# A transformer block on one core: where the first projections get their normalized rows, and when

## The chip, the cores and the metric

The kernel runs on one core of one Trainium2 chip. Its engines are TensorE (PE, matmuls; PEld is its weight load), VectorE (DVE), ScalarE (ACT), GpSimd (POOL) and SyncE (SP, which here only issues DMAs). The metric is device time in microseconds (us), the median of several executions; lower is better.

## What is computed

A layer norm of x (2048 rows of 448) feeds two branches whose sums are added to x: attention with 16 heads of 28 columns that share one k and one v, and an MLP with a hidden width of 1792.

```python
xn = _layernorm(x, axis=-1)                     # (x - mean) / sqrt(var + 1e-5)
q = (xn @ wq).reshape(B, S, 16, 28).transpose(0, 2, 1, 3)
k, v = xn @ wk, xn @ wv                         # one head for all
p = softmax(einsum("bhqd,bkd->bhqk", q, k) * 28 ** -0.5)
o = einsum("bhqk,bkd->bhqd", p, v).transpose(0, 2, 1, 3).reshape(B, S, 448)
return x + o @ wo + relu(xn @ w1) @ w2
```

## The kernel before

All arithmetic is in 32 bits. Most matmul operands are split into a high and a low part of TensorE's rounded 32-bit format (names that end in H and L, or hi and lo), and a product is the sum of three of the four partial products.

The 2048 rows are taken as four blocks of 512 (NQB = 4), each of four tiles of 128 rows (TPB). The kernel runs in three stages, one after the other: first layer norm and the q, k and v projections of the four blocks, then the MLP (from L436 on), then attention (from L593 on). The change lies in the first stage, L76 to L320. For a block b that stage does this:

- moments(b) (L196): DVE takes mean and variance of the four x tiles in acc, by four pairs of instructions (L200, L201).
- rstd(b) (L204): ACT takes a square root (L208), and DVE makes 1/sqrt(variance) from it in six small instructions (L209 to L214); nb, the last one, is what ACT's normalization adds.
- normalized_x(b) (L217): the four tiles are normalized, tiles 0 and 2 on DVE (L229), tiles 1 and 3 on ACT (L227). POOL copies the last 64 columns of each a second time (L232), which only the last chunk's transposes need.
- transposed(b) (L236): PE transposes the block, chunk by chunk (DC = 3 chunks of 128 columns and the doubled rest of 64; four transposes for a chunk, L241), into PSUM tiles named d, of which there are three, and o for the rest. ACT copies each chunk out as its high part xH (L243), DVE subtracts to get the low part xL (L244); the rest goes to xR by two copies on ACT and a subtraction on DVE (L247 to L249).
- qkv_proj(b, g) for four groups of heads g (L258): eleven matmuls of 512 columns (L187, L192) into a PSUM tile named a, of which there are four; then qkv_out (L251): ACT copies the result (L254), DVE subtracts (L255), and SP writes it to a scratch tensor in HBM (L256).

Block 0 is treated on its own: qkv_first (L263) does its four groups side by side in 44 matmuls, pass by pass through the chunks (L271), the passes with low weights last, and only then the four qkv_out. Its weights come from HBM as they are (wq by L116 to L120, wk and wv by L118 to L120, all issued by SP) and are split on the chip: high parts on ACT (split_hi, L146), low parts on POOL for chunks 0 and 2 and on DVE for chunks 1 and 3 (split_lo, L151).

While PE has no data, 28 warm-up matmuls of an identity run on it (L97; each stands as two instructions in the trace).

The order in which the functions are called in L278 to L319 is written out by hand, and it sets the order of the instructions of every engine. Before the change, block 1's moments, rstd and normalized_x are called ahead of qkv_first, and transposed(1) behind it. In the loop over b, moments(b + 1) stands ahead of the block's first projection, rstd(b + 1) behind it, normalized_x(b + 1) behind the second, transposed(b + 1) behind the third. SP issues the four tiles of block 0, then wq, wk, wv, then the twelve remaining x tiles (L137), and later the first MLP weights (load_part, L155), which POOL splits (split_part, L165) during block 2.

Of the kernel before, what the change touches and what calls it, by code (L numbers as in the profile page):

```python
# [8 lines left out]
F32 = mybir.dt.float32  # L9
F32R = mybir.dt.float32r  # L10
I32 = mybir.dt.int32
AF = mybir.ActivationFunctionType
ALU = mybir.AluOpType
# [25 lines left out]
def program(ctx: ExitStack, tc: tile.TileContext, HM, fine, x, wq, wk, wv, wo, w1, w2, out):  # L39
    nc = tc.nc  # L40
    P = 128
    S, D = x.shape
# [19 lines left out]
    WARM = 28  # L62
# [32 lines left out]
    pw = psD.tile([P, QB], F32, name="d")  # L95
# [16 lines left out]
    def chunks_in(dst, src, each=False):  # L112

        if each:
            for c in range(DC):
                nc.sync.dma_start(dst[:, c], src[c * P : (c + 1) * P])  # L116
        else:
            nc.sync.dma_start(dst[:, 0:DC], src[0 : DC * P].rearrange("(c p) n -> p c n", p=P))  # L118
        nc.sync.dma_start(dst[0:DR, DC], src[DC * P : D])
        nc.sync.dma_start(dst[DR:P, DC], src[DC * P : D])  # L120
# [9 lines left out]
    with nc.allow_non_contiguous_dma(reason="narrow k and v projections"):  # L130
        chunks_in(kvs[:, :, 0:DH], wk)
        chunks_in(kvs[:, :, DH : 2 * DH], wv)
# [11 lines left out]
    def split_hi(c, kv):  # L144
        src, hi, lo = wqkv_parts(c, kv)
        nc.scalar.activation(hi, src, AF.Copy)  # L146

    def split_lo(c, kv):
        src, hi, lo = wqkv_parts(c, kv)
        eng = nc.vector if c % 2 else nc.gpsimd  # L150
        eng.tensor_tensor(lo, src, hi.bitcast(F32), op=ALU.subtract)  # L151
# [42 lines left out]
    stat = {}  # L194

    def moments(b):  # L196
        mv = small.tile([P, TPB, 2], F32, name="mv")
        for i in range(TPB):
            st = small.tile([P, 6], F32, name="st")
            nc.vector.bn_stats(st, acc[:, b * TPB + i, :])  # L200
            nc.vector.bn_aggr(mv[:, i, :], st)  # L201
        stat[b] = mv

    def rstd(b):  # L204

        mv = stat[b]
        ve, sd, r0, t0, rs, nb = (small.tile([P, TPB], F32, name=k) for k in ("ve", "sd", "r0", "t0", "rs", "nb"))
# [7 lines left out]
        stat[b] = mv, rs, nb  # L215

    def normalized_x(b):  # L217

        mv, rs, nb = stat.pop(b)
        xn = []  # L220
        for i in range(TPB):
            if i % 2 == 0:
                pair = hpool.tile([P, FC, QB], F32, name="hL" if i else "hH")
            n = pair[:, i % 2]
            a = acc[:, b * TPB + i, :]
            if i % 2:
                nc.scalar.activation(n[:, 0:D], a, AF.Identity, bias=nb[:, i : i + 1], scale=rs[:, i : i + 1])  # L227
            else:
                nc.vector.tensor_scalar(  # L229
                    n[:, 0:D], a, mv[:, i, 0:1], rs[:, i : i + 1], op0=ALU.subtract, op1=ALU.mult  # L230
                )
            nc.gpsimd.tensor_scalar(n[:, D : D + DR], n[:, DC * P : D], 1.0, 0.0, op0=ALU.mult, op1=ALU.add)  # L232
            xn.append(n)
        return xn

    def transposed(b, xn, chunks=range(DC + 1)):  # L236
        xs = slice(b * QB, (b + 1) * QB)
        for c in chunks:
            pt = psD.tile([P, QB], F32, name="d") if c < DC else psO.tile([P, QB], F32, name="o")
            for i in range(TPB):  # L240
                nc.tensor.transpose(pt[:, i * P : (i + 1) * P], xn[i][:, c * P : (c + 1) * P], ident)  # L241
            if c < DC:
                nc.scalar.activation(xH[:, c, xs], pt, AF.Copy)  # L243
                nc.vector.tensor_tensor(xL[:, c, xs], pt, xH[:, c, xs].bitcast(F32), op=ALU.subtract)  # L244
            else:
                tmp = small.tile([P, QB], F32R, name="tmp")
                nc.scalar.activation(xR[0:DR, xs], pt[0:DR], AF.Copy)  # L247
                nc.scalar.activation(tmp[DR:P], pt[DR:P], AF.Copy)
                nc.vector.tensor_tensor(xR[DR:P, xs], pt[DR:P], tmp[DR:P].bitcast(F32), op=ALU.subtract)  # L249
# [31 lines left out]
    split_hi(1, False)  # L281
    xn = normalized_x(0)
    split_hi(0, True)
    split_hi(1, True)
    split_lo(1, False)
    split_lo(1, True)
    transposed(0, xn, (0, 1))
    split_hi(2, False)
    split_hi(2, True)
    transposed(0, xn, (2, 3))  # L290
    split_hi(3, False)
    split_hi(3, True)
    for c in (0, 2, 3):
        split_lo(c, False)
        split_lo(c, True)
    moments(1)
    rstd(1)
    xn = normalized_x(1)
    qkv_first(range(NHG))
    g0 = load_part(0)  # L300
    g1 = load_part(1)
    transposed(1, xn)
    for b in range(1, NQB):
        if b + 1 < NQB:
            moments(b + 1)
        qkv_proj(b, 0)
        if b + 1 < NQB:
            rstd(b + 1)
        qkv_proj(b, 1)
        if b + 1 < NQB:  # L310
            xn = normalized_x(b + 1)
        else:
            nc.scalar.activation(warm, eps_t, AF.Exp)
        qkv_proj(b, 2)
        if b + 1 < NQB:
            transposed(b + 1, xn)
        if b == 2:
            split_part(0, g0)
        qkv_proj(b, 3)  # L319
# [340 lines left out]
```

## Time and profile before

| | us |
|---|---|
| median of 3 runs | 883.08 (882.75 to 883.5) |
| the profiled execution, its own time | 882.62 |
| its span, first to last instruction | 880.8 |
| first stage, to the first MLP matmul | 58.83 |

The profile is of one execution. In its timeline a row is: start in us, busy time in us, engine, line, operation, output <- input, shapes, count, and in brackets the idle time of that engine just before and what ended it. SPq is SP's queue of DMA issues. In the table of windows a row is: the window, its length, then for each engine busy us and the number of instructions, then the granted clock of TensorE, the busy share of the DMA engines and GB/s. In a row of groups the figures behind the bar are busy us in total and mean ns of one. Matmuls are pipelined; where the text follows PE closely it goes by the starts of its weight loads (PEld).

### The profile page before, as it was taken

To read this page: it belongs to the slowest core of one execution; us is meant where nothing else is said; L and a number is where in the kernel's file an instruction comes from. 1 tells how busy PE (TensorE), PEld (TensorE's weight loads), DVE (VectorE), ACT (ScalarE), POOL (GpSimd) and SP (SyncE) were. 2 spreads that over 40 slices of the span, in tenths; PEclk is the share of its full clock that TensorE was granted. 3 is DMA by queue.
4 is the path that set the end of the run, shared out by engine and by line. 5 is a ranking of instruction groups with operands and counts; after the bars stand their busy time and mean duration, and the time that the engine had idled before them with its cause. 6 is when DMAs were issued, how large, how long until landed. Compare 5 with 4: busy or idle time off the path is not lost.

```text
span 880.8 us, 12946 instructions
## 1 busy us (share of the span) xinstructions
PE 871.0 (99%) x4998; PEld 573.0 (65%) x4998; DVE 471.0 (53%) x848; ACT 562.2 (64%) x871; POOL 113.3 (13%) x96
## 2 busy tenths in 40 slices
PE   9999999999999999999999999999999999999996
PEld 8788888888888886454554554554554554554562
DVE  6833344333333346474574574574574574574563
ACT  4541111111111116999999999999999999999993
POOL 3034202020202003010110110110110110110110
PEclk9999999999999999999999999999999999999998
DMA  6868050010000001020120230120230120230001
GB/s 214 293 200 167 4 132 23 23 45 1 1 1 1 0 2 38 2 56 25 33 56 21 57 77 21 36 56 20 58 77 15 42 56 17 62 77 14 2 13 46
DMA packets 37502, 45.89 MB, mean 52 GB/s; under 512 B 13640, under 2 KB 24072, under 8 KB 37264
## 3 DMA queue, kind: packets, MB, share of 16 engines
q1 hardware_dynamic: 37432, 44.98, 19.7%
q8 instruction: 41, 0.67, 0.3%
q14 instruction: 29, 0.24, 0.1%
HBM read 32.37 MB, written 12.18 MB: 51 GB/s over the span
## 4 chain that ended last, share of the span: by engine, by line
PE 98%; DVE 1%; ACT 1%; issue 0%; POOL 0%; POOLq 0%
PE o L477 25%; PE a L588 19%; PE a L187 16%; PE a L423 12%; PE d L588 10%; PE d L522 4%; PE o L423 4%; PE a L192 4%; PE d L370 2%; PE a L271 1%; PE d L97 1%; PE d L241 1%; ACT p L623 0%; PE a L565 0%; DVE qs L255 0%
## 5 line engine op out<-in xcount | busy, mean ns | idle before, releaser
L610 DVE COPY p<-d 128x512 f32<-128x512 f32 x384 | 246.1, 686 | 161.7 <-PE d L588 142.1
L605 ACT ACTIVATE p<-a 128x512 f32<-128x512 f32 x640 | 317.1, 708 | 21.7 <-PE a L588 21.7
L477 PE MATMUL o<-p,vtile 128*32 128x512 f32 x2048 | 229.5, 594 | 0.0
L588 PE MATMUL a<-qst,kst 114*128 114x512 f32 x640 | 225.4, 407 | 0.0
L410 ACT ACTIVATE hH<-a 128x512 fp32r<-128x512 f32 x56 | 33.5, 598 | 235.9 <-PE a L192 235.9
L623 ACT ACTIVATE p<-p 128x2048 f32<-128x2048 f32 x96 | 183.1, 2131 | 0.0
L588 PEld LDWEIGHTS a<-qst,kst 114*128 114x128 f32 x640 | 120.0, 187 | 77.2 <-ACT p L605 28.1
L477 PEld LDWEIGHTS o<-p,vtile 128*32 128x32 f32 x2048 | 61.6, 109 | 144.1 <-issue 128.3
L588 PE MATMUL d<-qst,kst 114*128 114x512 f32 x384 | 145.8, 400 | 0.0
L187 PE MATMUL a<-xH,w 128*128 128x512 f32 x408 | 104.8, 392 | 0.2 <-ACT xH L243 0.2
L411 DVE SCALAR_TENSOR_TENSOR hL<-a,hH 128x512 fp32r<-128x512 f32 x56 | 38.7, 692 | 118.4 <-ACT hH L410 118.4
L423 PE MATMUL a<-w,hH 128*128 128x448 f32 x336 | 95.6, 366 | 0.0
L187 PEld LDWEIGHTS a<-xH,w 128*128 128x128 f32 x408 | 76.1, 188 | 16.5 <-ACT xH L243 0.8
L588 PEld LDWEIGHTS d<-qst,kst 114*128 114x128 f32 x384 | 72.4, 188 | 12.9 <-DVE p L610 4.5
L508 POOL TENSOR_TENSOR on<-rb,oS 128x512 f32<-128x512 f32 x15 | 19.4, 1290 | 448.4 <-DMA rb<-rscr 418.0
L430 DVE TENSOR_TENSOR acc<-a,acc 128x448 f32<-128x448 f32 x84 | 52.2, 622 | 33.7 <-PE a L423 33.7
L423 PEld LDWEIGHTS a<-w,hH 128*128 128x128 f32 x336 | 63.0, 188 | 6.3
L423 PE MATMUL a<-w,hL 128*128 128x448 f32 x168 | 61.2, 364 | 0.0
L187 PE MATMUL a<-xL,w 128*128 128x512 f32 x204 | 57.7, 390 | 0.1
L187 PEld LDWEIGHTS a<-xL,w 128*128 128x128 f32 x204 | 38.3, 188 | 8.8 <-DVE xL L244 0.7
L192 PE MATMUL a<-xR,w 128*128 128x512 f32 x136 | 42.0, 390 | 0.2 <-DVE xR L249 0.2
L524 DVE TENSOR_TENSOR acc<-d,acc 128x448 f32<-128x448 f32 x60 | 37.3, 622 | 5.3 <-PE d L522 5.3
(111 smaller groups left out, 577.4 us busy)
## 6 DMA issues: line engine op xcount, KB each, us to landing
qst<-qscr SPq DMA_DIRECT2D x64, 224.0 KB
qscr<-qs SPq DMA_DIRECT2D x16, 512.0 KB
rb<-rscr SPq DMA_DIRECT2D x60, 64.0 KB
acc<-in_A_x SPq DMA_DIRECT2D x16, 224.0 KB
out<-acc SPq DMA_DIRECT2D x16, 224.0 KB
stg<-in_B_w SPq DMA_DIRECT2D x7, 448.0 KB
stg<-in_B_w SPq DMA_DIRECT2D x7, 384.0 KB
qst<-rows SPq DMA_DIRECT2D x128, 2.0 KB
```

The costliest lines, as they stand in the source:

```text
L187: nc.tensor.matmul(ps, lhs[:, wi, c, cols], xm[:, c, xs], start=n == 0, stop=False)
L192: nc.tensor.matmul(ps, lhs[:, wi, DC, cols], xR[:, xs], start=False, stop=wi == 1)
L411: nc.vector.scalar_tensor_tensor(hL[:, f], ph, 0.0, hH[:, f].bitcast(F32), op0=ALU.max, op1=ALU.subtract)
L423: nc.tensor.matmul(py[:, 0:D], hm[:, f, i * P : (i + 1) * P], wd[:, wi, f, :], start=n == 0, stop=n == 3 * FC - 1)
L430: nc.vector.tensor_tensor(acc[:, t, :], py[:, 0:D], acc[:, t, :], op=ALU.add)
L477: nc.tensor.matmul(o_acc[u][32 * j : 32 * j + 32], vtile[:, kb, :], p[:, j], start=start, stop=stop)
L522: nc.tensor.matmul(py, om[:, c], wm[:, g, :], start=n == 0, stop=n == 2)
L524: nc.vector.tensor_tensor(acc[:, t, :], py, acc[:, t, :], op=ALU.add)
L588: nc.tensor.matmul(pt, kst[0 : KQ + 2, kb * P : (kb + 1) * P], qst[u][0 : KQ + 2, j, :], start=True, stop=True)
L605: nc.scalar.activation(p, pt, AF.Exp, scale=SCALE)
L610: nc.vector.tensor_copy(p, pt)
L623: nc.scalar.activation(ps[kb], ps[kb], AF.Exp, scale=SCALE)
```

## The change

- wk and wv are loaded by issues on ACT's queue, behind ACT's first instruction; wq stays on SP.
- 24 warm-up matmuls instead of 28, and they write to a PSUM tile named a instead of d.
- Block 0's tiles are normalized by DVE, ACT, DVE and POOL; the second copies of the 64 last columns come behind all four. The high part of wq's chunk 1 is made on DVE instead of ACT, and all low parts on POOL, behind block 0's transposes in the code. The high parts of chunks 2 and 3 are made between the chunks of block 0's transposes.
- Block 1's moments, rstd and normalized_x are called behind qkv_first instead of ahead of it, right before its transposed(1). Then come the loads of the first MLP weights and moments(2), rstd(2).
- In the loop, normalized_x(b + 1) stands ahead of the block's first projection, transposed(b + 1) behind the second, and behind that moments(b + 2) and rstd(b + 2).

transposed is cut into x_bank, turn and split_x, with the same instructions; the small tiles of the statistics are allocated in moments.

```diff
--- before.py
+++ after.py
@@ -59,7 +59,7 @@
     W2C = FC * D
     SCALE = float(DH) ** -0.5
     EPS = 1e-5
-    WARM = 28
+    WARM = 24
     KQ = 4 * DH
     NU = NQB * NHG
     NA, ND, NST = 4, 3, 3
@@ -92,7 +92,7 @@
     gone = cst.tile([P, TPB + 3], F32, name="gone")
     nc.vector.memset(gone, 1.0)
 
-    pw = psD.tile([P, QB], F32, name="d")
+    pw = psA.tile([P, QB], F32, name="a")
     for _ in range(WARM):
         nc.tensor.matmul(pw[:, 0:P], ident, ident, start=True, stop=True)
     kst = cst.tile([P, S], F32R, name="kst")
@@ -109,15 +109,15 @@
     proj_scope = ExitStack()
     npool = proj_scope.enter_context(tc.tile_pool(name="npool", bufs=1, side="right"))
 
-    def chunks_in(dst, src, each=False):
+    def chunks_in(dst, src, each=False, eng=nc.sync):
 
         if each:
             for c in range(DC):
-                nc.sync.dma_start(dst[:, c], src[c * P : (c + 1) * P])
+                eng.dma_start(dst[:, c], src[c * P : (c + 1) * P])
         else:
-            nc.sync.dma_start(dst[:, 0:DC], src[0 : DC * P].rearrange("(c p) n -> p c n", p=P))
-        nc.sync.dma_start(dst[0:DR, DC], src[DC * P : D])
-        nc.sync.dma_start(dst[DR:P, DC], src[DC * P : D])
+            eng.dma_start(dst[:, 0:DC], src[0 : DC * P].rearrange("(c p) n -> p c n", p=P))
+        eng.dma_start(dst[0:DR, DC], src[DC * P : D])
+        eng.dma_start(dst[DR:P, DC], src[DC * P : D])
 
 
     nc.scalar.activation(warm, eps_t, AF.Sqrt)
@@ -128,8 +128,8 @@
     kvs = stg[:, (DC + 1) * D : (DC + 1) * (D + 2 * DH)].rearrange("p (c n) -> p c n", c=DC + 1)
     chunks_in(s3, wq, each=True)
     with nc.allow_non_contiguous_dma(reason="narrow k and v projections"):
-        chunks_in(kvs[:, :, 0:DH], wk)
-        chunks_in(kvs[:, :, DH : 2 * DH], wv)
+        chunks_in(kvs[:, :, 0:DH], wk, eng=nc.scalar)
+        chunks_in(kvs[:, :, DH : 2 * DH], wv, eng=nc.scalar)
     wqkv = wpool.tile([P, 2, 4, 512], F32R, name="w")
     w4 = wqkv.rearrange("p s c (g n) -> p s c g n", g=NHG)
     nc.gpsimd.memset(w4[:, :, :, :, MQ + DHH : P].bitcast(F32), 0.0)
@@ -141,14 +141,16 @@
         cols = slice(MQ, MQ + DHH) if kv else slice(0, MQ)
         return src, w4[:, 0, c, :, cols], w4[:, 1, c, :, cols]
 
-    def split_hi(c, kv):
+    def split_hi(c, kv, eng=None):
         src, hi, lo = wqkv_parts(c, kv)
-        nc.scalar.activation(hi, src, AF.Copy)
+        if eng is None:
+            nc.scalar.activation(hi, src, AF.Copy)
+        else:
+            eng.tensor_copy(hi, src)
 
     def split_lo(c, kv):
         src, hi, lo = wqkv_parts(c, kv)
-        eng = nc.vector if c % 2 else nc.gpsimd
-        eng.tensor_tensor(lo, src, hi.bitcast(F32), op=ALU.subtract)
+        nc.gpsimd.tensor_tensor(lo, src, hi.bitcast(F32), op=ALU.subtract)
 
     parts = {}
 
@@ -191,20 +193,22 @@
         for wi in range(2):
             nc.tensor.matmul(ps, lhs[:, wi, DC, cols], xR[:, xs], start=False, stop=wi == 1)
 
-    stat = {}
+    stat, xns = {}, {}
 
     def moments(b):
-        mv = small.tile([P, TPB, 2], F32, name="mv")
+
+        stat[b] = tuple(
+            small.tile([P, TPB, 2] if k == "mv" else [P, TPB], F32, name=k)
+            for k in ("mv", "ve", "sd", "r0", "t0", "rs", "nb")
+        )
         for i in range(TPB):
             st = small.tile([P, 6], F32, name="st")
             nc.vector.bn_stats(st, acc[:, b * TPB + i, :])
-            nc.vector.bn_aggr(mv[:, i, :], st)
-        stat[b] = mv
+            nc.vector.bn_aggr(stat[b][0][:, i, :], st)
 
     def rstd(b):
 
-        mv = stat[b]
-        ve, sd, r0, t0, rs, nb = (small.tile([P, TPB], F32, name=k) for k in ("ve", "sd", "r0", "t0", "rs", "nb"))
+        mv, ve, sd, r0, t0, rs, nb = stat[b]
         nc.scalar.activation(sd, mv[:, :, 1], AF.Sqrt, bias=eps_t)
         nc.vector.tensor_scalar(ve, mv[:, :, 1], EPS, None, op0=ALU.add)
         nc.vector.reciprocal(r0, sd)
@@ -212,41 +216,50 @@
         nc.vector.tensor_tensor(t0, t0, ve, op=ALU.mult)
         nc.vector.scalar_tensor_tensor(rs, t0, 1.5, r0, op0=ALU.add, op1=ALU.mult)
         nc.vector.scalar_tensor_tensor(nb, mv[:, :, 0], -1.0, rs, op0=ALU.mult, op1=ALU.mult)
-        stat[b] = mv, rs, nb
-
-    def normalized_x(b):
-
-        mv, rs, nb = stat.pop(b)
-        xn = []
-        for i in range(TPB):
-            if i % 2 == 0:
-                pair = hpool.tile([P, FC, QB], F32, name="hL" if i else "hH")
-            n = pair[:, i % 2]
+
+    def normalized_x(b, by=(nc.vector, nc.scalar) * 2):
+
+        mv, rs, nb = stat[b][0], stat[b][5], stat[b][6]
+        xns[b] = [hpool.tile([P, FC, QB], F32, name=k) for k in ("hH", "hL")]
+        for i, eng in enumerate(by):
+            n = xns[b][i // 2][:, i % 2]
             a = acc[:, b * TPB + i, :]
-            if i % 2:
-                nc.scalar.activation(n[:, 0:D], a, AF.Identity, bias=nb[:, i : i + 1], scale=rs[:, i : i + 1])
+            if eng is nc.scalar:
+                eng.activation(n[:, 0:D], a, AF.Identity, bias=nb[:, i : i + 1], scale=rs[:, i : i + 1])
             else:
-                nc.vector.tensor_scalar(
+                eng.tensor_scalar(
                     n[:, 0:D], a, mv[:, i, 0:1], rs[:, i : i + 1], op0=ALU.subtract, op1=ALU.mult
                 )
+        for i in range(TPB):
+            n = xns[b][i // 2][:, i % 2]
             nc.gpsimd.tensor_scalar(n[:, D : D + DR], n[:, DC * P : D], 1.0, 0.0, op0=ALU.mult, op1=ALU.add)
-            xn.append(n)
-        return xn
-
-    def transposed(b, xn, chunks=range(DC + 1)):
+
+    def x_bank(c):
+        return psD.tile([P, QB], F32, name="d") if c < DC else psO.tile([P, QB], F32, name="o")
+
+    def turn(b, c, pt):
+
+        for i in range(TPB):
+            n = xns[b][i // 2][:, i % 2]
+            nc.tensor.transpose(pt[:, i * P : (i + 1) * P], n[:, c * P : (c + 1) * P], ident)
+
+    def split_x(b, c, pt):
+
         xs = slice(b * QB, (b + 1) * QB)
-        for c in chunks:
-            pt = psD.tile([P, QB], F32, name="d") if c < DC else psO.tile([P, QB], F32, name="o")
-            for i in range(TPB):
-                nc.tensor.transpose(pt[:, i * P : (i + 1) * P], xn[i][:, c * P : (c + 1) * P], ident)
-            if c < DC:
-                nc.scalar.activation(xH[:, c, xs], pt, AF.Copy)
-                nc.vector.tensor_tensor(xL[:, c, xs], pt, xH[:, c, xs].bitcast(F32), op=ALU.subtract)
-            else:
-                tmp = small.tile([P, QB], F32R, name="tmp")
-                nc.scalar.activation(xR[0:DR, xs], pt[0:DR], AF.Copy)
-                nc.scalar.activation(tmp[DR:P], pt[DR:P], AF.Copy)
-                nc.vector.tensor_tensor(xR[DR:P, xs], pt[DR:P], tmp[DR:P].bitcast(F32), op=ALU.subtract)
+        if c < DC:
+            nc.scalar.activation(xH[:, c, xs], pt, AF.Copy)
+            nc.vector.tensor_tensor(xL[:, c, xs], pt, xH[:, c, xs].bitcast(F32), op=ALU.subtract)
+        else:
+            tmp = small.tile([P, QB], F32R, name="tmp")
+            nc.scalar.activation(xR[0:DR, xs], pt[0:DR], AF.Copy)
+            nc.scalar.activation(tmp[DR:P], pt[DR:P], AF.Copy)
+            nc.vector.tensor_tensor(xR[DR:P, xs], pt[DR:P], tmp[DR:P].bitcast(F32), op=ALU.subtract)
+
+    def transposed(b):
+        for c in range(DC + 1):
+            pt = x_bank(c)
+            turn(b, c, pt)
+            split_x(b, c, pt)
 
     def qkv_out(b, g, pq):
         xs = slice(b * QB, (b + 1) * QB)
@@ -278,44 +291,45 @@
     moments(0)
     rstd(0)
     split_hi(0, False)
-    split_hi(1, False)
-    xn = normalized_x(0)
+    normalized_x(0, (nc.vector, nc.scalar, nc.vector, nc.gpsimd))
     split_hi(0, True)
     split_hi(1, True)
-    split_lo(1, False)
-    split_lo(1, True)
-    transposed(0, xn, (0, 1))
-    split_hi(2, False)
-    split_hi(2, True)
-    transposed(0, xn, (2, 3))
-    split_hi(3, False)
-    split_hi(3, True)
-    for c in (0, 2, 3):
+    split_hi(1, False, nc.vector)
+    for c in range(DC + 1):
+        pt = x_bank(c)
+        turn(0, c, pt)
+        split_x(0, c, pt)
+        if c in (0, 1):
+            split_hi(c + 2, False)
+            split_hi(c + 2, True)
+    for c in range(DC + 1):
         split_lo(c, False)
         split_lo(c, True)
-    moments(1)
-    rstd(1)
-    xn = normalized_x(1)
     qkv_first(range(NHG))
-    g0 = load_part(0)
-    g1 = load_part(1)
-    transposed(1, xn)
     for b in range(1, NQB):
+        if b == 1:
+            moments(1)
+            rstd(1)
+            normalized_x(1)
+            transposed(1)
+            g0 = load_part(0)
+            g1 = load_part(1)
+            moments(2)
+            rstd(2)
         if b + 1 < NQB:
-            moments(b + 1)
+            normalized_x(b + 1)
+        else:
+            nc.scalar.activation(warm, eps_t, AF.Exp)
         qkv_proj(b, 0)
-        if b + 1 < NQB:
-            rstd(b + 1)
         qkv_proj(b, 1)
         if b + 1 < NQB:
-            xn = normalized_x(b + 1)
-        else:
-            nc.scalar.activation(warm, eps_t, AF.Exp)
-        qkv_proj(b, 2)
-        if b + 1 < NQB:
-            transposed(b + 1, xn)
+            transposed(b + 1)
+        if b + 2 < NQB:
+            moments(b + 2)
+            rstd(b + 2)
         if b == 2:
             split_part(0, g0)
+        qkv_proj(b, 2)
         qkv_proj(b, 3)
     proj_scope.close()
 
```

## The prediction

> **What bounds the kernel now.** I read the page first: the engine totals, then the chain that ended last.
>
> ```profile
> PE 871.0 (99%) x4998; PEld 573.0 (65%) x4998; DVE 471.0 (53%) x848; ACT 562.2 (64%) x871; POOL 113.3 (13%) x96
> ...
> PE 98%; DVE 1%; ACT 1%; issue 0%; POOL 0%; POOLq 0%
> ```
>
> TensorE (PE) holds 98% of the chain. Whatever makes PE wait is paid in full; whatever another engine does in PE's shadow is free. The diff touches only the time before the MLP, so next I cut the span at the places where PE goes from one kind of work to the next, in the table of windows.
>
> ```profile
> 11.74:21.55 9.81, 9.81 (x46) 8.15 (x44) 8.03 (x23) 4.95 (x12) 2.68 (x7) 1.00 0.76 258
> 21.55:58.83 37.28, 36.63 (x182) 29.58 (x181) 26.28 (x59) 20.88 (x38) 8.13 (x11) 1.00 0.72 251
> ```
>
> The first row is qkv_first (44 matmuls), the second is blocks 1 to 3 (twelve projections, three sets of sixteen transposes) up to the first MLP matmul at 58.83. How little of the second row is waiting shows from the undisturbed pieces in the timeline:
>
> ```profile
> 44.59 0.37 PEld L241 LDWEIGHTS d<-ident,hH 128*128 128x128 f32 x2
> ...
> 46.45 1.23 PEld L187 LDWEIGHTS a<-xH,w 128*128 128x128 f32 x6
> ...
> 53.84 1.32 PEld L187 LDWEIGHTS a<-xH,w 128*128 128x128 f32 x6
> ...
> 58.83 1.32 PEld L187 LDWEIGHTS a<-xH,w 128*128 128x128 f32 x6
> ```
>
> A set of transposes is 46.45 - 44.59 = 1.86 us; 53.84 to 58.83 holds two projections, so 2.495 each. 12 x 2.495 + 3 x 1.86 = 35.5 of 37.28: blocks 1 to 3 contain 1.8 us of waits. That is the most this part of the change could win.
>
> **In what order the engines work.** Everything below rests on one question: does an engine take instructions in the order of the code? VectorE (DVE) answers it in block 1 to 2:
>
> ```profile
> 38.21 0.69 DVE L255 TENSOR_TENSOR qs<-a,qs 128x512 fp32r<-128x512 f32 x1 [1.16 <-ACT qs L254]
> ...
> 38.82 0.62 DVE L200 BATCH_NORM_STATS2 st<-acc 128x6 f32<-128x448 f32 x1
> ```
>
> DVE idled 1.16 us for a projection's output (L255), although the next block's statistics (L200) needed only x, which had long been in SBUF. They stand after that L255 in the code, and they ran after it. So order in the code is order on the engine.
>
> **The moved statistics of block 1: the main term.** Before, moments(1), rstd(1) and normalized_x(1) stand ahead of qkv_first. After, they stand behind it, and so behind its four qkv_out, whose copies and subtractions wait for qkv_first's last matmuls.
>
> ```profile
> 18.32 0.18 DVE L201 BATCH_NORM_AGGREGATE mv<-st 128x2 f32<-128x6 f32 x1
> ...
> 20.53 0.75 ACT L227 ACTIVATE hL<-acc,nb,rs 128x448 f32<-128x448 f32 x1
> 20.68 0.87 PEld L271 LDWEIGHTS a<-xR,w 128*128 128x128 f32 x4
> ...
> 21.33 2.06 ACT L254 ACTIVATE qs<-a 128x512 fp32r<-128x512 f32 x4
> ...
> 21.59 0.37 PEld L241 LDWEIGHTS d<-ident,hH 128*128 128x128 f32 x2
> ...
> 21.96 2.48 DVE L255 TENSOR_TENSOR qs<-a,qs 128x512 fp32r<-128x512 f32 x4 [1.28 <-ACT qs L254]
> ...
> 27.00 0.63 DVE L200 BATCH_NORM_STATS2 st<-acc 128x6 f32<-128x448 f32 x1
> ...
> 29.84 0.18 DVE L201 BATCH_NORM_AGGREGATE mv<-st 128x2 f32<-128x6 f32 x1
> ```
>
> Now: block 1 is normalized at 21.28 (20.53 + 0.75), under the matmuls, and PE passes from qkv_first (20.68 + 0.87 = 21.55) straight to the transposes at 21.59. I call 21.33, where ScalarE (ACT) takes the first finished projection, E. After the change the links from E run in series:
>
> - DVE's four subtractions end at 21.96 + 2.48 = 24.44, E + 3.11.
> - moments(1) (eight instructions, 27.00 to 30.02 in the next block): 3.02, so E + 6.13.
> - rstd(1) and the four normalizations, from the last aggregate's end (18.50) to ACT's last tile (21.28): 2.78, so E + 8.91.
>
> PE stands still from E + 0.22 to about E + 8, against nothing now.
>
> **Block 2, which now comes behind two projections instead of three.** More rows, from block 0's transposes and block 2's splits:
>
> ```profile
> 9.54 0.75 ACT L227 ACTIVATE hL<-acc,nb,rs 128x448 f32<-128x448 f32 x1
> ...
> 10.34 0.14 PEld L241 LDWEIGHTS d<-ident,hL 128*128 128x128 f32 x1 [0.18 <-ACT hL L227]
> ...
> 10.82 1.06 ACT L243 ACTIVATE xH<-d 128x512 fp32r<-128x512 f32 x2
> ...
> 11.71 2.59 PEld L271 LDWEIGHTS a<-xH,w 128*128 128x128 f32 x12
> ```
>
> ```profile
> 33.68 1.58 ACT L243 ACTIVATE xH<-d 128x512 fp32r<-128x512 f32 x3
> ...
> 36.35 0.69 DVE L249 TENSOR_TENSOR xR<-o,tmp 64x512 fp32r<-64x512 f32 x1
> ```
>
> From the last normalized tile (10.29) to the first copy out of the transposes (10.82) is at most 0.53; I take 0.48: E + 9.39. From there to the end of the last split, 33.68 to 37.04, is 3.36: E + 12.75. DVE then does moments(2), 3.02, and rstd(2) with normalized_x(2), 2.78: E + 18.55. PE meanwhile ends its transposes at 8.91 + 0.05 + 1.37 (10.34 to 11.71) = E + 10.33, and two projections, with about 0.35 of waiting for the last split, at E + 15.7. It waits some 2.9 us for block 2's tiles: the third projection that covered this now comes behind. The transposes end at 18.55 + 0.05 + 1.37 = E + 19.97. What PE still has is ten projections and block 3's transposes, 24.95 + 1.86: E + 46.78.
>
> Is block 3 late too? PE reaches it at E + 19.97 + 9.98 = E + 29.95. After block 2's tiles ACT must first do the two queued copies (L254, 2.06 / 4 = 0.5 each), so the splits start at E + 19.6 and end at 22.9, moments(3) at 26.0, and rstd, two held L255 of 0.69 and the normalizations end near E + 29.8 to 30.1. It just fits; 0 to 0.4 us, taken as 0. POOL's weight split for the MLP (L168) follows block 3's tiles at about 51 us and has until 67 us.
>
> **The start.**
>
> ```profile
> 1.36 8.71 PE L97 MATMUL d<-ident 128*128 128x128 f32 x56 [1.36 <-POOL ident masks.py:199]
> ...
> 2.03 0.20 ACT L123 ACTIVATE warm<-eps_t 128x1 f32<-128x1 f32 x1
> ...
> 5.26 0.59 SPq L118 DMA_DIRECT2D stg<-in_A_wk  x1
> ...
> 7.22 0.30 ACT L208 ACTIVATE sd<-mv,eps_t 128x4 f32<-128x4 f32 x1 [4.98 <-DVE mv L201]
> ...
> 8.35 0.16 DVE L214 SCALAR_TENSOR_TENSOR nb<-mv,rs 128x4 f32<-128x4 f32 x1
> ...
> 8.85 0.51 DVE L229 TENSOR_SCALAR hL<-acc,mv,rs 128x448 f32<-128x448 f32 x1
> ...
> 9.61 6.44 SPq L137 DMA_DIRECT2D acc<-in_A_x  x12
> ...
> 10.57 1.39 POOL L151 TENSOR_TENSOR w<-stg,w 128x448 fp32r<-128x448 f32 x2
> ...
> 11.78 0.71 ACT L146 ACTIVATE w<-stg 128x448 fp32r<-128x448 f32 x2
> ...
> 12.38 0.59 ACT L243 ACTIVATE xH<-d 128x512 fp32r<-128x512 f32 x1
> ```
>
> ```profile
> 20.95 0.24 POOL L232 TENSOR_SCALAR hL<-hL 128x64 f32<-128x64 f32 x1
> ```
>
> Tile 3's normalization goes from ACT (end 10.29) to POOL. POOL's price for 448 columns lies between 0.24 (64 columns) and 1.39 (a 448-column and a 56-column subtraction together); I take 0.6, since the operation is of L232's kind, and it then ends near 9.0. ACT's one tile starts at nb (8.51), no longer behind wq's second chunk, and ends near 9.3; DVE's second ends at 9.36. Four warm-ups fewer (8 of 56 rows, at the late rate of about 0.1 each) free PE near 9.1. So the transposes end some 0.8 earlier. But the third pass of qkv_first needs xH's third chunk, and ACT now does, from 9.87 (9.36 and the 0.5 of above), a copy (0.53, half of the 1.06 for two), a weight pair (0.71), a copy, a pair and a copy (0.59): 12.94, as good as the present 12.97. The third pass started at about 13.45 (eight matmuls of 0.22 after 11.71), so the gain at E is about 0.45, and 0.05 if POOL takes its dear end.
>
> Wk and wv: six issues move from SP to ACT, at 0.59 each 3.5 us after 2.23, so to about 5.8; ACT is idle until 7.22, which covers it (at 0.85 an issue the cover would be gone and each 0.1 more costs 0.6). On SP the twelve x tiles move up from 9.61 to about 5.3; nobody waits for them now. The wk and wv bytes, about 115 KB with the doubled rows, now fall among the first x tiles:
>
> ```profile
> 5.00:6.00 1.00, 1.00 (x7) 1.00 (x7) 1.00 0.90 323
> 6.00:7.00 1.00, 1.00 (x11) 1.00 (x10) 1.00 0.93 344
> ```
>
> With the DMA engines 90% busy at 323 GB/s they delay the x tiles by 0 to 0.7 (115 KB / 323 GB/s, doubled for their short rows); I take 0.2. [...] The weight subtractions all on POOL are four pairs of 1.39 from about 10.4, so to 16; they are first needed near 17.5 and cost nothing.
>
> **Sum.** E moves to 21.33 - 0.45 + 0.2 = 21.08. The MLP starts at 21.08 + 46.78 = 67.86 instead of 58.83: 9.0 us later. The MLP and attention are PE-bound and untouched, so nothing gives it back. The profiled execution took 882.62 with a span of 880.8; that gives 891.6. The median of the three runs is 0.46 higher, 883.08, and I forecast 892.1 for it.
>
> **Rivals.** *The clock falls in the new gap.* The two rows of warm-up matmuls above show 7 per us until 6 us and 11 after (the granted clock reads 1.00 in both): PE starts slow for about 4.6 us. A gap of 8 us may bring that back. Right after the first gap it is mostly free, since PE then has 2.9 us to spare before block 2. If it strikes after block 2's wait, where PE is the bound again, it costs 4.6 x (1 - 7/11) = 1.7 us: 893.8. Against it: that second gap is short. [...] No wait in this trace is long enough to test it.
>
> *The order is not that of the code.* If the statistics of block 1 were taken under qkv_first all the same, where DVE has idle time ahead of 21.96, the gap vanishes, E gains 0.25 and up to 1.8 of the present waits could go: 881.0 to 882.8 in medians, faster or no change. It decides if DVE's L200 of block 1 starts before L255 of block 0. Against it: the 1.16 us idle row. The same numbers hold if the diff did not do what its words say.
>
> *ACT's issues become the bound.* At 1.2 us an issue they end at 9.4 and hold back L208 by 2.2: 894.3. The 0.59 of SP's row speaks against it.
>
> **Chances.** Forecast 0.77, clock 0.13, ACT's issues 0.05, order 0.05, the last split between same (0.03) and faster (0.02). A measurement of this kernel can tell about 0.2%, 1.8 us, from no change. Slower 0.95, same 0.03, faster 0.02. For the range I take the low ends of the start (0.2), and 1.2 for the two chains' links being shorter where they follow directly, with some room: 889.8; upward 0.4 for POOL, 0.5 for DMA, 0.4 for block 3 and 1.7 for the clock: 895.1.
>
> **What would show it.** In the changed profile: DVE's L255 of block 0 ahead of moments(1); PE idle some 8 us near 21 to 29, ended by the normalization, and again 2 to 3 us ahead of block 2's transposes; none ahead of block 3's; the first MLP matmul near 67.9; the rest of the span as long as now (880.8 - 58.83 = 822 us). I am wrong if moments(1) lies before 21 us, if the rate of 7 per us returns for projections, or if ACT's sqrt of block 0 is later than 7.9.

## The result and the profile after

The changed kernel takes 897.06 us (median of 5 runs, 895.51 to 897.57) against 883.08: ratio 1.0153, interval 1.014 to 1.0167. It is slower by 14.0 us where 9.0 were forecast, and it lies above the range. The profiled execution took 895.61, its span is 893.7.

The page of after, engine totals and chain:

```profile
PE 872.7 (98%) x4990; PEld 574.5 (64%) x4990; DVE 471.3 (53%) x845; ACT 561.1 (63%) x869; POOL 117.3 (13%) x101
...
PE 95%; DVE 1%; ACT 1%; DMA 1%; issue 0%; POOL 0%; SPq 0%; ACTq 0%; DVEq 0%
```

PE's work is what it was, but PE holds 95% of the chain, not 98%: a part of the chain now passes through other engines. The timeline of after shows where:

```profile
21.37 1.07 PE L284 MATMUL a<-xR,w 128*128 128x512 f32 x4
21.80 2.06 ACT L267 ACTIVATE qs<-a 128x512 fp32r<-128x512 f32 x4 [6.83 <-PE a L284]
22.43 2.48 DVE L268 TENSOR_TENSOR qs<-a,qs 128x512 fp32r<-128x512 f32 x4 [6.74 <-ACT qs L267]
...
24.83 0.61 DVE L206 BATCH_NORM_STATS2 st<-acc 128x6 f32<-128x448 f32 x1
...
29.71 0.49 PEld L244 LDWEIGHTS d<-ident,hH 128*128 128x128 f32 x2 [7.70 <-issue]
...
30.67 0.18 PEld L244 LDWEIGHTS d<-ident,hL 128*128 128x128 f32 x1 [0.36 <-ACT hL L228]
...
31.19 0.60 ACT L250 ACTIVATE xH<-d 128x512 fp32r<-128x512 f32 x1 [0.56 <-PE d L244]
...
32.04 0.60 ACT L250 ACTIVATE xH<-d 128x512 fp32r<-128x512 f32 x1 [0.26 <-PE d L244]
...
34.98 0.69 DVE L256 TENSOR_TENSOR xR<-o,tmp 64x512 fp32r<-64x512 f32 x1 [0.76 <-ACT tmp L255]
...
40.73 0.14 PEld L244 LDWEIGHTS d<-ident,hH 128*128 128x128 f32 x1 [2.11 <-issue]
...
40.94 0.75 ACT L228 ACTIVATE hL<-acc,nb,rs 128x448 f32<-128x448 f32 x1
...
69.72 1.32 PEld L189 LDWEIGHTS a<-xH,w 128*128 128x128 f32 x6
```

DVE was idle for 6.74 us under qkv_first, and took block 1's statistics (L206) only behind the four L268. PE stood still for 7.70 us and again for 2.11 ahead of block 2's transposes. The first MLP matmul comes at 69.72 instead of 58.83, 10.89 later. The span is 12.9 longer, so 2 us were lost behind it. The last arithmetic instruction and the span, of before and of after:

```profile
874.12 0.14 DVE L571 TENSOR_SCALAR fine<-d 1x1 int32<-1x1 f32 x1
...
core 0: 880.8 us, clock 0.997
```

```profile
885.05 0.13 DVE L585 TENSOR_SCALAR fine<-d 1x1 int32<-1x1 f32 x1
...
core 0: 893.7 us, clock 0.993
```

In after it ends at 885.18, and 8.5 us follow; in the kernel before it ends at 874.26, and 6.5 follow. The granted clock, the column behind POOL's, in windows of after:

```profile
26.00:28.00 2.00, 0.00 (x0) 0.00 (x0) 1.86 (x7) 0.12 (x1) 0.00 (x0) 0.86 1.02 375
28.00:30.00 2.00, 0.26 (x1) 0.18 (x1) 1.70 (x8) 0.97 (x3) 0.32 (x1) 0.50 1.02 291
30.00:32.00 2.00, 2.00 (x9) 1.62 (x9) 0.20 (x2) 1.22 (x2) 0.77 (x4) 0.50 1.07 279
32.00:34.00 2.00, 2.00 (x11) 1.90 (x10) 1.68 (x3) 1.45 (x3) 0.00 (x0) 0.50 0.91 272
34.00:36.00 2.00, 2.00 (x10) 1.66 (x9) 1.21 (x3) 0.93 (x2) 0.00 (x0) 0.93 1.09 324
```

The clock is at half from about 27.4 to 34.3. The theory that I tested: the order of the statistics costs about 9 us as forecast, and the other 5 are the half clock, POOL's tile and the end of the program. The rivals: the loss comes from the start or from the loop's order, or the half clock is covered.

### The profile page after: what moved, and what is told of

It is laid out like the page before. It is cut to its first block, busy times and chain, and to the rows that moved or that the text cites. A ratio compares the mean times of both kernels' runs of the same rounds, so it can differ in the third digit from the quotient of the medians.

```text
span 893.7 us, 12931 instructions
## 1 busy us (share of the span) xinstructions
PE 872.7 (98%) x4990; PEld 574.5 (64%) x4990; DVE 471.3 (53%) x845; ACT 561.1 (63%) x869; POOL 117.3 (13%) x101
## 4 chain that ended last, share of the span: by engine, by line
PE 95%; DVE 1%; ACT 1%; DMA 1%; issue 0%; POOL 0%; SPq 0%; ACTq 0%; DVEq 0%
PE o L491 25%; PE a L602 18%; PE a L189 15%; PE a L437 11%; PE d L602 10%; PE d L536 4%; PE o L437 4%; PE a L194 3%; PE d L384 2%; PE a L284 1%; PE d L244 1%; DVE st L206 0%; DMA acc<-in_A_x 0%; ACT p L637 0%; PE a L579 0%
```

## The experiments

**e1: only block 1's statistics moved, in the kernel before.**

```diff
-    moments(1)
-    rstd(1)
-    xn = normalized_x(1)
     qkv_first(range(NHG))
+    moments(1)
+    rstd(1)
+    xn = normalized_x(1)
```

> Kernel before with one edit: moments, rstd and normalized_x of block 1 are called behind qkv_first. Theory (the moved statistics are the main cost): PE idles 7 to 8 us behind qkv_first, ended by the normalization, the clock falls to half in that gap, the first MLP matmul comes at 67 to 68 instead of 58.83, time 891 to 893.5. Rival (the loss comes from the start and from the loop's order, and the moved statistics are covered): within 2 us of the kernel before, 882.5 to 885.

890.93 us, ratio 1.0092 (1.0075 to 1.0109). PE's waits of e1 in the first 75 us, total, times and longest:

```profile
PE d L241 <- DVE hH L229: 7.3, 1, 7.3
```

The first MLP matmul comes at 67.27, and the granted clock is at half here too, for 6.8 us from 26.9 on. The time lies just under the expected 891. Moving three calls costs 8 us by itself; the rival falls.

**e2: the same three calls put back ahead of qkv_first, in the kernel after.**

```diff
+    moments(1)
+    rstd(1)
+    normalized_x(1)
     qkv_first(range(NHG))
...
-            moments(1)
-            rstd(1)
-            normalized_x(1)
             transposed(1)
```

> Kernel after with one edit undone: moments, rstd and normalized_x of block 1 are called ahead of qkv_first again. Theory: the 7.3 us gap and the half clock are gone; what stays is 0.5 at the start, 2 to 3 us of waiting ahead of block 2's transposes, which come behind two projections, and 2 us behind the last arithmetic: 886.5 to 889, all runs within 1 us. Rival (loop's order and start are the cost): 893 or more.

889.41 us, ratio 1.0077 (1.006 to 1.0093): 7.65 less than after, but 6.5 above before, and a little more than expected. The executions lie 1.7 us apart, not within 1. The 7.7 us gap is gone. What I had not expected is a fall of the clock behind the wait ahead of block 2's transposes, in the timeline and the windows of e2:

```profile
32.77 0.14 PEld L244 LDWEIGHTS d<-ident,hH 128*128 128x128 f32 x1 [2.18 <-issue]
```

```profile
30.00:32.00 2.00, 1.00 (x5) 0.50 (x3) 1.61 (x8) 0.30 (x1) 0.00 (x0) 1.00 1.01 280
32.00:34.00 2.00, 1.16 (x4) 0.60 (x5) 1.04 (x4) 1.67 (x3) 0.99 (x4) 0.81 0.88 270
34.00:36.00 2.00, 2.00 (x11) 2.00 (x11) 1.62 (x3) 1.82 (x5) 0.05 (x1) 0.50 1.10 335
36.00:38.00 2.00, 2.00 (x10) 1.76 (x9) 1.46 (x3) 1.75 (x3) 0.00 (x0) 0.84 1.05 363
```

Ahead of block 2's transposes PE waits 2.2 us (the cover of the third projection is gone), and then the clock is at half for 3.4 us, where PE is the bound again. The rival of the prediction that I had called unlikely occurs here, in a gap that I had called short. But the length of the gap does not decide it. The waits at the same place in after (2.11, at 40.73) and in e4 below (2.18) left the clock at full. The windows of after, and the wait of e4:

```profile
38.00:40.00 2.00, 1.05 (x5) 0.54 (x3) 1.60 (x8) 0.30 (x1) 0.00 (x0) 1.00 0.00 0
40.00:42.00 2.00, 1.00 (x5) 0.61 (x6) 1.01 (x3) 1.71 (x3) 1.02 (x4) 1.00 0.00 0
```

```profile
39.38 0.14 PEld L244 LDWEIGHTS d<-ident,hH 128*128 128x128 f32 x1 [2.18 <-issue]
```

The stretches of half clock in the first stage are 3.4 us long in e2, 6.8 in after and e1, and 10.2 in e7 (below). What decides whether the clock falls behind such a wait, no run here shows.

**e3: wk and wv on SP again, in the kernel after.**

```diff
-        chunks_in(kvs[:, :, 0:DH], wk, eng=nc.scalar)
-        chunks_in(kvs[:, :, DH : 2 * DH], wv, eng=nc.scalar)
+        chunks_in(kvs[:, :, 0:DH], wk)
+        chunks_in(kvs[:, :, DH : 2 * DH], wv)
```

> Kernel after with wk and wv issued by SP again. Theory (SP's shorter instruction stream puts a code load into its last instructions): the stretch from the last arithmetic instruction to the end of the span is 6.5 us again instead of 8.5, the start is within 0.5, time 893 to 895.5. Rival (that stretch is longer because of the clock or of the output's transfer): 8.5 us again, time 895.5 to 897.5.

894.0 us (893.36 to 895.89), 3.1 less than after. The last arithmetic instruction of e3, and its span:

```profile
885.07 0.14 DVE L585 TENSOR_SCALAR fine<-d 1x1 int32<-1x1 f32 x1
...
core 0: 891.6 us, clock 0.994
```

The work ends within 0.05 of after's 885.18, and 6.4 us follow instead of 8.5. E is at 22.03, and E less the start of block 0's square root is 14.39 against 14.40 in after. So the second queue did nothing that shows for the first stage, and with the six issues off SP 2 us more follow at the far end. The trace's records of SP in that stretch (start in us) tell where: in after its semaphore waits, one each 0.08 us, stop in the middle for 2.2 us, and in that time instructions are transferred.

```
after  889.91  SP wait, L34
after  889.98  SP wait, L34
       890.06 to 890.22  four transfers of instructions, 8 KB each; one of 16 KB at 891.18
after  892.15  SP wait, L34
after  892.25  SP wait, L34
```

The pause stands behind the fifth of these waits in every profile in which SP had lost the six issues (after, e2, e4, e5, e6, e7, g4; 2.0 to 3.3 us), and in no other profile. That the transfers make it is not shown: in the kernel before four of 8 KB each start among the same run of waits, from 878.78 to 879.30, and the waits go on without a pause (0.10 from one to the next at most).

**e4: matmuls in the gap, in the kernel after.**

```diff
         if b == 1:
+            pk = psO.tile([P, QB], F32, name="o")
+            for _ in range(34):
+                nc.tensor.matmul(pk[:, 0:P], ident, ident, start=True, stop=True)
             moments(1)
```

> Kernel after with 34 matmuls of the identity (as in the warm-up) put on PE behind qkv_first, in the gap. They compute nothing that is used. Theory (the half clock after the gap stretches block 1's transposes and splits, and the number of half-clock windows differs between executions): clock 1.00 all through the first stage, block 1's last split 1 us earlier, first MLP matmul at about 68.6, time 894 to 894.7 and all runs within 0.7 us of each other. Rival (the half clock is covered by the wait for block 2): 895.5 to 897.5 with the same spread of 2 us.

The windows of e4:

```profile
28.00:30.00 2.00, 2.00 (x20) 1.88 (x19) 1.68 (x7) 0.96 (x3) 0.40 (x2) 1.00 1.02 285
30.00:32.00 2.00, 1.79 (x17) 1.55 (x16) 0.42 (x1) 1.58 (x4) 0.69 (x4) 1.00 0.97 284
32.00:34.00 2.00, 2.00 (x12) 1.57 (x9) 1.84 (x4) 1.58 (x4) 0.00 (x0) 1.00 0.94 263
```

The clock stays at 1.00, and the first MLP matmul comes at 68.38, 1.34 earlier than in after. Counted from E it is 46.68 against 47.92 in after. With the half clock the other profiles have the same as after (e3 47.88, e7 47.88, g4 47.91), without it h1 has 46.60. So the half clock was not covered; it cost 1.2 to 1.3 us. The time, 895.45 (895.09 to 897.11), is above what I expected and just under the rival's range, since the end grew again: SP's pause is 3.26 us here, at the same place, and 10.1 us follow the last arithmetic. The spread stayed too: the execution of 897.11 had a lower clock (0.994) than the others (0.996 and 0.997).

**e5 and e7: POOL's tile.** e5 gives POOL constants in place of the columns of mean and rstd, so it leaves block 0's last tile unnormalized; e7 gives the tile back to ACT.

```diff
-    normalized_x(0, (nc.vector, nc.scalar, nc.vector, nc.gpsimd))
+    normalized_x(0)
```

> Kernel after with POOL's normalization of block 0's last tile given the constants 0 and 1 instead of the two columns of mean and rstd, so that this one tile goes unnormalized into the rest. Theory (the columns as operands make the instruction dear): it falls from 2.08 us to 0.4 to 0.7, and E, ScalarE's first copy of a finished projection, comes 0.8 to 1 us earlier than in the kernel after. Rival (POOL is slowed by VectorE working at the same time): 1.5 us or more again.

> Kernel after with block 0's last tile back on ScalarE. Theory (POOL's 2.08 us set the start): E at 20.8 to 21.2 instead of 21.8, and everything behind it earlier by as much, time 895.5 to 896.8 in the median. Rival (the start is set by the weight pairs on ScalarE, which now wait longer): E at 21.6 or later, 896.8 to 897.6.

POOL's tile in after, and in e5:

```profile
8.61 2.08 POOL L230 TENSOR_SCALAR hL<-acc,mv,rs 128x448 f32<-128x448 f32 x1 [6.30 <-DMA stg<-in_A_wq]
```

```profile
6.78 1.71 POOL L231 TENSOR_SCALAR hL<-acc 128x448 f32<-128x448 f32 x1 [4.46 <-DMA acc<-in_A_x]
```

At most 0.37 of the 2.08 is due to the columns: the expectation of 0.4 to 0.7 fell, and the rival's number came, which h2 below tells apart from its reason (e5's one time is 894.85, its E is at 21.15, 0.65 earlier than in after). In e7, 895.77 us, E is at 21.30, 0.5 earlier than in after though not at the 20.8 to 21.2 expected. E itself moves from profile to profile with the start of block 0's square root (6.89 to 8.18 over the profiles), so the fair measure is E less that start. The ACT rows of before, after and e7:

```profile
7.22 0.30 ACT L208 ACTIVATE sd<-mv,eps_t 128x4 f32<-128x4 f32 x1 [4.98 <-DVE mv L201]
...
21.33 2.06 ACT L254 ACTIVATE qs<-a 128x512 fp32r<-128x512 f32 x4
```

```profile
7.40 0.30 ACT L212 ACTIVATE sd<-mv,eps_t 128x4 f32<-128x4 f32 x1 [5.17 <-DVE mv L207]
```

```profile
7.46 0.30 ACT L212 ACTIVATE sd<-mv,eps_t 128x4 f32<-128x4 f32 x1 [5.23 <-DMA stg<-in_A_wv]
...
21.30 2.06 ACT L267 ACTIVATE qs<-a 128x512 fp32r<-128x512 f32 x4 [6.82 <-PE a L284]
```

That is 14.11 before, 14.40 after and 13.84 in e7. Over the profiles it is 14.37 to 14.40 with the tile on POOL (after, e2, e3, e4, g4), 13.82 to 14.12 with the new start and the tile on ACT (e7, e8, g1, h1), and 13.80 to 14.20 with the old start (before, e1, e6, g2, g3), but 14.52 in h2, whose start is the old one too. (In e5, whose tile waits for no statistics, it is 13.40.) So within the new start the tile on POOL loses 0.3 to 0.6, and the rest of the new start wins nothing that shows. Against the old start the loss is not shown beyond the spread.

**g4: an early tensor_scalar of one column on POOL, in the kernel after**, for the idea that POOL's first one is dear.

```diff
     nc.gpsimd.memset(w4[:, :, :, :, MQ + DHH : P].bitcast(F32), 0.0)
+    pwarm = cst.tile([P, 1], F32, name="pwarm")
+    nc.gpsimd.tensor_scalar(pwarm, eps_t, eps_t, eps_t, op0=ALU.subtract, op1=ALU.mult)
```

> Kernel after with one tensor_scalar of one column put on POOL behind its memsets, before the x tiles land. It computes nothing that is used. Theory (POOL's first tensor_scalar pays 0.73 us, as L232's first of 0.97 against 0.24 in the kernel before): the tile takes 1.3 to 1.4 us instead of 2.08, E 0.6 to 0.7 us earlier than 21.8, time 896.2 to 896.6 in the median. Rival (448 columns with two column operands cost 2.08 by themselves): 2.0 to 2.1 again, E as before, 895.5 to 897.6.

The tile takes 2.10 us, the time is 896.48. That theory fell.

**h2: POOL's prices by themselves**, nine probes in the kernel before, three of each kind.

```diff
+            for _ in range(3):
+                nc.gpsimd.tensor_scalar(
+                    pout, pin[:, 0:D], eps_t, eps_t, op0=ALU.subtract, op1=ALU.mult
+                )
+            for _ in range(3):
+                nc.gpsimd.tensor_scalar(pout, pin[:, 0:D], 0.0, 1.0, op0=ALU.subtract, op1=ALU.mult)
+            for _ in range(3):
+                nc.gpsimd.tensor_scalar(pout, pin[:, 0:D], 1.0, 0.0, op0=ALU.mult, op1=ALU.add)
```

> Kernel before with nine probe instructions on POOL during the MLP, when VectorE is idle two thirds of the time; they read a constant tile of 448 columns and their result isn't used: three with two column operands (subtract, multiply), three with constants (subtract, multiply), three with constants (multiply, add). Theory (the column operands and the operation make the price, wherever it runs): about 2.1, 1.7 and 0.5 us. Rival (the start of the kernel makes it, where VectorE and the transfers are busy): under 0.8 us for all.

Its groups (busy us, mean ns):

```profile
L446 POOL TENSOR_SCALAR pout<-vtile,eps_t 128x448 f32<-128x448 f32 x3 | 5.6, 1861 | 0.2
L450 POOL TENSOR_SCALAR pout<-vtile 128x448 f32<-128x448 f32 x3 | 5.1, 1711 | 0.3
L452 POOL TENSOR_SCALAR pout<-vtile 128x448 f32<-128x448 f32 x3 | 1.7, 566 | 0.2
```

The pair of operations makes the price: subtract and multiply 1.71, multiply and add 0.57, the columns 0.15 more, a little less than expected. With columns the price at the kernel's start is another 0.2 higher (2.08 in after, 2.10 in g4); with constants it is 1.71 there too (e5). (The kernel's own 891.54 says nothing: the probes held up POOL's weight split behind them, which starts at 95.00 instead of 81.68.)

**e6 and g3: wk and wv on ACT alone, in the kernel before (e6), and with six small loads on SP that give its stream the old length (g3).**

```diff
     for t in range(TPB, NT):
         nc.sync.dma_start(acc[:, t, :], xv[:, t, :])
+    pad = cst.tile([P, 6, DH], F32, name="pad")
+    with nc.allow_non_contiguous_dma(reason="as wk and wv"):
+        for i in range(6):
+            nc.sync.dma_start(pad[:, i], wk[0:P])
```

> Kernel before with one edit: wk and wv are issued by ScalarE. Theory (it does nothing for the start, and SP's stream, six issues shorter, runs into a code load in its last instructions): E within 0.3 of 21.33, 8 to 10 us instead of 6.5 from the last arithmetic instruction to the end, time 884.5 to 886.5. Rival (the second queue is a gain or harmless): 882 to 883.5.

> Kernel e6_kv_on_act (before with wk and wv issued by ScalarE) with six small loads put on SP behind the x tiles; they load 128 rows of wk into a tile that nobody reads. SP's stream has its old length again. Theory (the length of SP's stream decides where its last instructions stand, and those run into a code load): the 2 us pause among SP's last semaphore waits is gone, 6.3 to 6.6 us from the last arithmetic instruction to the end, time 882.3 to 883.5. Rival (the pause comes from ScalarE's queue being in use): 8 us or more again, 885 to 886.

e6: 886.0 us, ratio 1.0033 (1.002 to 1.0046), slower. g3: 883.16, ratio 1.0003 (0.9994 to 1.0012), no change. The last arithmetic instruction and span of e6, then the last arithmetic of g3, whose span is 881.1:

```profile
873.51 0.13 DVE L571 TENSOR_SCALAR fine<-d 1x1 int32<-1x1 f32 x1
...
core 0: 881.8 us, clock 0.998
```

```profile
874.68 0.14 DVE L575 TENSOR_SCALAR fine<-d 1x1 int32<-1x1 f32 x1
```

8.2 us follow in e6, 6.3 in g3, where ACT's queue is used as much. So the end goes with SP's six issues, not with the queue that wk and wv take. E came at 20.71 in e6, 0.6 earlier than before where at most 0.3 was expected, and at 21.93 in g3, whose wk and wv take the same way; so this is not the queue either. (e6's profiled execution took 883.61 and the four others 885.7 to 886.1, with a clock of 0.995 or 0.996 against 0.998; what the others lost besides the 1.7 of this pause has no profile.)

**e8 and g1: a version from what was learned.** From after: wk and wv on SP, the tile on ACT, block 1's statistics ahead of qkv_first, and in the loop

```diff
         if b + 1 < NQB:
+            moments(b + 1)
+            rstd(b + 1)
             normalized_x(b + 1)
...
         qkv_proj(b, 0)
         qkv_proj(b, 1)
+        qkv_proj(b, 2)
         if b + 1 < NQB:
             transposed(b + 1)
```

g1 is e8 with 28 warm-ups.

> A version from what the runs show: kernel after with wk and wv on SP, block 0's last tile on ScalarE, block 1's statistics and normalization ahead of qkv_first, the transposes behind the third projection as before, and rstd and normalized_x of the next block ahead of the block's first projection. Theory (only what stands ahead of a covered wait may be moved): no clock drop, E near 21, no wait ahead of the transposes of blocks 2 and 3, 881 to 882.5. Rival (DVE has no room, what is won ahead of block 2 is lost at block 1's projections): 883 to 884.

> Kernel e8_covered with 28 warm-up matmuls instead of 24. Theory (24 are too few to bring the clock up in every execution, and those that miss pay one more half-clock stretch of 3.4 us, about 1.8 us): no execution is 1.5 us above the others any more, median 882 to 882.6. Rival (the two groups of times come from the end of the program): a third of the executions near 884.3 again.

e8: 882.91 (882.14 to 884.6), ratio 1.0003 (0.9994 to 1.0012); 4 of 11 executions lie at 884.1 to 884.6, with a clock of 0.995 or 0.996 where the others have 0.997 to 0.999. g1: 882.58, none above 883.23, ratio 0.9997 (0.9988 to 1.0006). e8 is above its expectation of 881 to 882.5, g1 within its own. No loss is left, but no gain that can be measured.

**g2: 24 warm-ups in the kernel before.**

```diff
-    WARM = 28
+    WARM = 24
```

> Kernel before with 24 warm-up matmuls instead of 28, nothing else. Theory (the same): some executions 1.5 to 2 us above the others, those with the lower granted clock; the others within 0.5 of the kernel before, whose tiles set the start anyway. Rival: all executions within 882.3 to 883.8, as the kernel before.

882.91 (882.69 to 883.44), ratio 1.0 (0.9991 to 1.0009), one group. Fewer warm-ups do no harm in this order of the code. Whether they made e8's second group was not shown: it is 4 of 11 executions against none of 11 in g1, and e6, with 28 warm-ups, has such executions too.

**h1: after with the three found costs out, and 28 warm-ups.** wk and wv on SP, the tile on ACT, 28 warm-ups, e4's matmuls, and ten more ahead of block 2's transposes:

```diff
         qkv_proj(b, 1)
+        if b == 1:
+            pk = psO.tile([P, QB], F32, name="o")
+            for _ in range(10):
+                nc.tensor.matmul(pk[:, 0:P], ident, ident, start=True, stop=True)
```

> Kernel after with the three unforecast costs taken out together: wk and wv on SP again, block 0's last tile on ScalarE again, 28 warm-ups, and matmuls of the identity in both gaps (34 behind qkv_first, 10 ahead of block 2's transposes; they compute nothing that is used). What is left of the change is the order of the statistics and of the transposes. Theory (order 9 us, the rest is clock, POOL's tile and the end of the program): 891 to 892.4, all executions within 1 us, clock never low before the end, 6.3 to 6.6 us behind the last arithmetic. Rival (something else, in particular the 2 us between groups of executions, belongs to the order itself): 893 or more, or executions 1.5 us apart.

892.41 us, all within 892.06 to 892.62, ratio 1.0106 (1.0089 to 1.0123): at the top of what was expected, and within 0.3 of the forecast's 892.1 with the order of the calls alone. 6.7 us follow the last arithmetic, a little more than expected. 4.65 of after's 14.0 are the rest. The first MLP matmul of h1:

```profile
68.21 1.32 PEld L189 LDWEIGHTS a<-xH,w 128*128 128x128 f32 x6
```

From E (21.61) to it h1 takes 46.60, where the prediction had worked out 46.78. That the time meets the forecast so closely is in part luck, since E is 0.5 later than the 21.08 of the sum.

## Why the prediction missed

- The order of the engines, the two series of links and where PE waits: right. Link by link after has E + 3.11 (24.91), 6.04 (27.84), 8.83 (30.63), 9.39 (31.19) for E + 3.11, 6.13, 8.91, 9.39. e1 and h1 show that this is the main cause. From E to the first MLP matmul it is 37.50 before and 46.60 in h1, so the order costs 9.1 where the prediction had 9.28 (46.78 less 37.50).
- The half clock: "Right after the first gap it is mostly free" is a step that failed. I set it against PE's 2.9 us to spare before block 2, but the slow transposes stretch the chain that sets that wait: ACT's copies come 0.85 apart instead of 0.53, and block 1's last split ends at 35.67, E + 13.87 instead of 12.75. DVE's moments(2) stand behind it, so block 2 comes later too: its last tile is normalized at 41.69, E + 19.89 instead of 18.55. At full clock the links come out as predicted, E + 12.62 and 18.65 in e4, E + 12.60 and 18.56 in h1. So the half clock costs 1.2 to 1.3 that the sum had at nothing. The clock is at half for 6.8 us in after, 3.4 in e2, 10.2 in e7. The slow stretch that the rival took as 4.6 us is 3.4 long in e2, so at half clock it can cost at most 1.7 there.
- The start: the term for x (0.2 taken, 0.18 measured, from the starts of the square root) came out by luck: with wk and wv on SP that start lies anywhere from 7.14 to 8.18, with them on ACT from 6.89 to 7.75, so no profile can tell the term. That transfers of short rows take about twice the time shows in the kernel before: from 8 to 9 us, where 703 of 738 packets are under 512 B, the DMA engines move 135 GB/s at a busy share of 0.85, against 333 at 0.92 from 5 to 7 us, with 45 of 417. The gain of 0.45 by earlier transposes does not show even with the tile on ACT. POOL's price was mis-sized: 0.6 taken, 1.39 the upper end, 2.08 measured, because I read it from L232, which multiplies and adds (0.57 for 448 columns in h2), and not from the pair of subtract and multiply that the tile needs (1.71). In place of the gain stands a loss: E less the start of the square root is 0.3 longer in after than before instead of 0.45 shorter. ACT's issues ended at 6.9 and not 5.8, and cost nothing.
- "the rest of the span as long as now" is the step that failed by most: by 2.0 us in the profile, through SP's pause. No rival had it; the section on the start counted what the six issues cost and not that they were taken out of a stream. A gain by the second queue does not show either: with wk and wv on ACT's queue and SP's stream at its old length the ratio is 1.0003 (g3).
- In sum, for the profiled executions: 9.0 forecast, 1.1 to 1.3 clock, 0.7 start, 2.0 end, 13.0 measured. The median lies 1.45 above the profiled execution, 1.0 more than in the kernel before. In h1 it is gone (its executions are within 0.6), with the three costs out and 28 warm-ups in; which of the four it belongs to was not separated, and stays open.

## What to carry to other kernels

Where engines take their instructions in the order of the code, a step that was hidden must stay ahead of the first instruction that waits for the work which hid it: three calls moved by one line cost 8 us, although VectorE stood idle for 6.7 us just ahead of the place they were moved to. A long wait of the matmul engine can also cost the slow clock behind it, even where that engine has time to spare, when other engines' links wait for its next results: here 6.8 us at half clock from within a wait of 7.7 us on, and 1.2 to 1.3 us lost. And a change of one engine's stream of DMA issues can change the end of the program: with six fewer on SP 8.5 us followed the last arithmetic instead of 6.5. Look at what follows it before explaining a difference of 2 us.

## What the runs showed of the hardware

- The clock fell to half for 3.4 us behind a wait of 2.2 us (e2), with transposes behind it, and not only in a wait of 7.7 (6.8 us at half in after). Behind waits of 2.1 and 2.2 us at the same place it did not fall (after, e4).
- SP's semaphore waits near the program's end stood still for 2.0 to 3.3 us in the kernels where SP had lost six issues, in after while instructions were transferred; where it had them, or six others, they did not.
- On POOL a subtract and multiply of 448 columns takes 1.71 us with constants, a multiply and add 0.57 (h2).
